# RWKV-7 attention and a hard-swish FFN on one core: three slots a unit on three PSUM pairs, with half turns

## The chip, the cores and the metric

The kernel runs on one NeuronCore of a Trainium2 chip. The metric is the device time of one launch in microseconds (us). Engines are named as in the profile: PE is TensorE's matmuls, PEld its weight loads, DVE VectorE, ACT ScalarE, POOL GpSimd, and SP the engine whose queue issues most DMAs.

## What is computed

All values are float32. The attention has B = 4, H = 8, T = 768 steps, D = 40, one 40 x 40 state for each batch row and head:

```python
for t in range(S):
    y[:, :, t] = np.einsum('bhd,bhde->bhe', rt, state)
    Sa = np.einsum('bhde,bhe->bhd', state, at)
    state_decay = state * wt[:, :, None, :] - np.einsum('bhd,bhe->bhde', Sa, bt)
    state = state_decay + np.einsum('bhd,bhe->bhde', vt, kt)
```

Its output, reordered to 3072 tokens x 320 features, goes through an FFN of width 2048:

```python
h = x @ w_in                       # 320 -> 2048
g = h * np.clip(h + 3.0, 0.0, 6.0) / 6.0
return g @ w_out                   # 2048 -> 320
```

## The kernel before

**Units.** The sequence is cut into chunks of 64 steps. A unit is 64 steps of two batch rows, with the two rows in the two halves of the 128 partitions: 24 units, 0 to 23, four to a group. Units i and i + 2 share a state. Each unit passes through two sets of stages. `prepare` doesn't need the state and runs ahead: W (turn the decays, scan them), gam (the second scan; factors gam and rgam), A, B and K (turn the input, multiply by a factor), F and E (products of these), factor (turn rgam, scale K and B on POOL), EV. `step` needs the state: RT, VT and S (turns of r, v and the state), R, U, UT, C, rS, H, then sn (the state's update) and y; move and move2 send y to the FFN's input xt by DMA. Once a group, `invert` inverts a triangular 32 x 32 system for all its heads on DVE, a chain of 60 small products and sums (L741, L747) between transposes (fb at the start, tb and tt at the end); `third_block` completes the inverse on PE (L776, L799).

**Turns.** A turn is a transpose on PE. `turn_pairs` (L474) does four 128 x 128 transposes into one bank; `turn_halves` (L484) does eight with 64 rows each, the two batch rows going to the two banks of a pair. From unit 8 on A, B, R, V and rgam (L643) are turned by halves, and W, K and the state (L878) are turned whole.

**FFN jobs.** A unit gives two jobs, (i, 0) and (i, 1), half of the hidden columns each. `expand` writes the hidden values to two banks "h" (L1054: 16 full 128-row products and 8 on half the rows, the "narrow" ones, issued by `short`). ACT (L1069) and DVE (L1070) make gt of them. `contract` (L1095) multiplies gt by w_out into the bank "o", 8 products of 320 columns. A float32 product leaves two records in the trace. The contract of a job is issued after the expand of the next job. The sum of a unit stays in "o" over both jobs, and ACT (L1113) copies it to ob once per unit, from where a DMA takes it out; units 0 and 1 are split into two sums.

**PSUM and order.** There are eight banks: "one" (1), "pair" (two pairs, 4), "o" (1), "h" (2). The order is written out by the program, with no scheduler behind it. From unit 4 on a unit has four blocks. In a block, `together` issues the PE products of all stages that are due, first for the state stages, then for those that run ahead, closing a batch (`finish`, which issues the copies out of PSUM on ACT and DVE) when five banks are in use. Between them `feed` issues pieces of the FFN: a piece is one step of the generator `feed_forward`, four FFN tiles of `expand` or two or so products of `contract`. While an inversion is open (`side`), `aside` issues two of its steps with each piece. Each engine executes its own list strictly in the order of issue.

Of the kernel before, what the change touches and what calls it, by code (L numbers as in the profile page):

```python
# [31 lines left out]
def kernel(  # L32
# [64 lines left out]
    def bank(tag, shape, bufs):  # L97
        return ps.tile(shape, F32, name=tag, tag=tag, bufs=bufs)

    ring, open_half = deque(), [None]  # L100
    lent = tc.tile_pool(name="lent", bufs=1, space=PSUM)
    pools = {"lent": lent.__enter__(), "pair": ps}
    pairs = deque([("pair", 2), ("pair", 2), ("lent", 1)])
# [7 lines left out]
    def begun_ffn():  # L111
# [4 lines left out]
        pools["h"] = ctx.enter_context(tc.tile_pool(name="hidden", bufs=1, space=PSUM))  # L116


    def ps_any(shape):
# [404 lines left out]
    def prepare(i, F):  # L524
        n, o = i % NU, data[i]
        halves = i >= 2 * NU
        def w_stage():
            wt = turn_pairs(o["WN"])
            yield PE

            wm = o["wm"] = wms[i % 2]
            wv = wm[:, 0:SCAN].rearrange("p (r m i) -> p r m i", m=2, i=HB + 1)
            x = wt[:].rearrange("p r (q m i) -> p (r q) m i", q=2, m=2)
            if i == 0:
                nc.vector.tensor_copy(wv[:, :, 0, 1:HB + 1], x[:, :, 0, ::-1])
            else:
                nc.scalar.activation(out=wv[:, :, 0, 1:HB + 1], in_=x[:, :, 0, ::-1], func=AF.Copy)
            if i == 0:
                nc.vector.tensor_copy(wv[:, :, 1, 1:HB + 1], x[:, :, 1, :])
            else:  # L540
                nc.scalar.activation(out=wv[:, :, 1, 1:HB + 1], in_=x[:, :, 1, :], func=AF.Copy)  # L541
            fetch("W", following(i))
            prods = o["prods"] = tmp.tile([P, NB, 2, HB + 1], F32, name="prods", bufs=2)
            nc.vector.tensor_tensor_scan(  # L544
                out=prods[:].rearrange("p r m i -> p (r m i)"), data0=wm[:, 0:SCAN], data1=start[:],
                initial=0.0, op0=ALU.mult, op1=ALU.add,
            )
# [89 lines left out]
        def factor_stage():  # L637
# [23 lines left out]
            for x, name in enumerate("KB"):  # L661
# [4 lines left out]
                )  # L666
            if i > 2 * NU:
                fetch("V", i)
# [3 lines left out]
        def k_stage():  # L672
            x = turn_pairs(o["KN"])
            yield PE
            kt = o["kt"] = turned("kt")
            nc.vector.tensor_tensor(out=kt[:], in0=x[:], in1=o["rg"][:], op=ALU.mult)

        def e_stage():
            x = scores(o["kt"], o["at"])
            yield PE  # L680
            o["E"] = masked(x)

        def ev_stage():
# [82 lines left out]
    def third_block(F, tb, tt, n, zs, first=False):  # L766


        parts = [slice(0, H)]
        zp = ps_pair(H, L)  # L770
        for h in range(H):
# [20 lines left out]
        shared[0] = None  # L792
        yield DONE
        tp = ps_pair(H, L)
        for h in range(H):
# [24 lines left out]
    def step(i):  # L820
# [52 lines left out]
        def s_S():  # L873

            sp = ps_any([P, 2, 2, P])
            for q in range(2):
# [171 lines left out]
    def expand(xt, j0, gts):  # L1048
# [9 lines left out]
        def short():  # L1058
            narrow.clear()
            for i in range(NQ):  # L1060
                for c in range(2):
                    add(c, i, win2[half(c), (j0 + i) * P:(j0 + i + 1) * P], xt[half(c), 2, :])
            if begun[0] + begun[1] == 6 * NQ:
                results()

        def results():
            for c in range(2):
                gt = ffn.tile([P, NQ, P], F32, name="gt", bufs=5)
# [6 lines left out]
        for c in range(2):  # L1075
            for t in range(2):
                for i in range(NQ):
                    j = c * HJ + j0 + i
                    add(c, i, win[:, t, j * P:(j + 1) * P], xt[:, t, :])
                if c == 1 and t == 1 and not narrow:  # L1080
                    results()
                yield True
        if not spread[0] and narrow:
# [3 lines left out]
    def contract(i, r, gts):  # L1087
        split = i < SPLIT
        if r == 0 or split:
            op = bank("o", [P, 512], 1)[:, 0:DM]  # L1090
        else:
            op = sums.pop(i)
        for c in range(2):
            for n in range(NQ):
                nc.tensor.matmul(out=op[:], lhsT=gts[c][:, n, :],  # L1095
                                 rhs=wout[:, c * HJ + r * NQ + n, :],
                                 start=((split or r == 0) and c == 0 and n == 0),
                                 stop=((split or r == 1) and c == 1 and n == NQ - 1))
                if n % 2 and (c == 0 or n < NQ - 1):
                    yield True  # L1100
        if r == 0:
            sums[i] = op
            if split:
                part = ffn.tile([P, 3 * P], F32, name="part", tag="xt", bufs=6)[:, 0:DM]
                nc.scalar.activation(out=part, in_=op[:], func=AF.Copy, scale=1.0 / 6.0)
                sums[i] = part
        else:
            ob = ffn.tile([P, DM], F32, name="ob", bufs=OB)
            if split:
                nc.vector.scalar_tensor_tensor(out=ob[:], in0=op[:], scalar=1.0 / 6.0,  # L1110
                                               in1=sums.pop(i), op0=ALU.mult, op1=ALU.add)
            else:
                nc.scalar.activation(out=ob[:], in_=op[:], func=AF.Copy, scale=1.0 / 6.0)  # L1113
            del ready[i]
            g, p = names[i]
            for q in range(2):
                row = (2 * p + q) * T + g * BL
                queue = nc.scalar if q and i == NK - 1 else nc.sync
                queue.dma_start(out=out[row:row + BL, :], in_=ob[half(q)])
        yield True  # L1120


    RGT, OB = 2, 1
    stream = feed_forward()
    weights = load_weights()
# [3 lines left out]
    def pieces(n):  # L1129

        owed[0] += n * (8 / 9 if spread[0] else 1)
        while owed[0] >= 1:
            owed[0] -= 1
            if not next(stream):
                owed[0] = 0.0
# [192 lines left out]
    def together(stages):  # L1328
# [3 lines left out]
        def finish():  # L1332
# [4 lines left out]
            begun.clear()  # L1337
            shared[0] = open_half[0] = None
            ring.clear()
            ring.extend(TURNS_IN)  # L1340

# [52 lines left out]

    m = 0
    for i in range(NU, NK):
        spread[0] = i >= 2 * NU - 1
        for j in range(BLOCKS):
            rate, inversion = 3.5, 0
            if i + AHEAD >= NK + NU - 1:  # L1400
                rate = 4.5
            if i < 2 * NU - 1:
                rate = 2.8
            parts = a_block(m)
            next(parts)
            if side or i % NU == NU - 1 and rate < 4:

                rate, inversion = 6.2, 2 + (i < 2 * NU)
            feed(rate / 2, inversion)
            for _ in parts:  # L1410
                pass
            if i % NU < 2 and j < 2:
                if i % NU == 0:
                    aside(3 * L)
                block(i, j)
            if side:
                rate, inversion = 6.2, 2 + (i < 2 * NU)
            feed(rate / 2, inversion)
            m += 1
    for _ in range(2):  # L1420
        for _ in a_block(m):
            pass
        m += 1
    spread[0] = False
# [32 lines left out]
```

## Time and profile before

| | us |
|---|---|
| median of 3 runs | 797.86 |
| lowest and highest | 796.54 to 798.12 |
| span of the profiled execution, first to last instruction | 802.0 |

The profile gives the profiled execution no time beside its span; the span is 4.1 us, 0.5%, over the median. Other rows that the steps use, of whole groups: L1054 busy 250.4 us, L1095 231.8 us, L1070 62.0 us (mean 681 ns), L555 37.6 us (1565 ns), L544 30.3 us (1270 ns), L520 49.9 us (723 ns), L1113 9.6 us (435 ns). Matmuls are pipelined: the mean of one L1054 record is 282 ns, but the next begins after some 112 ns, so costs on PE are read from starts, not from durations.

### The profile page before, as it was taken

How to read it: one execution, taken by the hardware profiler on the slowest of the kernel's cores; microseconds unless marked ns; L12 is line 12 of the kernel's file. 1: busy time of each engine (PE TensorE's matmuls, PEld its weight loads, DVE VectorE, ACT ScalarE, POOL GpSimd, SP SyncE). 2: the span in 40 equal slices, each digit the busy share in tenths (PEclk: the TensorE clock that was granted, in tenths of full speed). 3: DMA queues.
4: the chain of work that ended last, by engine and by line, in shares of the span. 5: the costliest groups of instructions: out<-in, count | busy, mean ns of one | idle time of the engine just before them, and what ended most of it. 6: DMA issues, size and time to landing. Idle time of an engine off the chain costs nothing.

```text
span 802.0 us, 35325 instructions
## 1 busy us (share of the span) xinstructions
PE 733.3 (91%) x15832; PEld 622.8 (78%) x15832; DVE 495.5 (62%) x967; ACT 321.2 (40%) x668; POOL 175.6 (22%) x318
## 2 busy tenths in 40 slices
PE   5726777999999989999999999999999999999998
PEld 4625665878778868888888888888888888888886
DVE  7896777679555699455698445897444973322210
ACT  2348882321644424543344453324443324422111
POOL 6403012420322222223123123304122202000000
PEclk9855798999999999999999999999999999999999
DMA  9683553420233331233222233213222101110000
GB/s 120 118 198 85 152 142 57 76 46 9 45 57 66 59 56 28 53 64 56 41 45 43 44 58 62 46 34 57 44 51 48 20 20 29 30 25 13 15 19 17
DMA packets 174215, 45.03 MB, mean 56 GB/s; under 512 B 157424, under 2 KB 172784, under 8 KB 174064
## 3 DMA queue, kind: packets, MB, share of 16 engines
q1 hardware_dynamic: 169760, 42.03, 27.7%
q8 instruction: 125, 2.05, 1.1%
q10 hardware_dynamic: 4304, 0.74, 0.7%
q14 instruction: 26, 0.21, 0.1%
HBM read 34.08 MB, written 3.93 MB: 47 GB/s over the span
## 4 chain that ended last, share of the span: by engine, by line
PE 77%; DVE 8%; issue 5%; DMA 4%; SPq 2%; ACT 2%; POOL 1%; DVEq 0%; ACTq 0%; POOLq 0%
PE h L1054 26%; PE o L1095 24%; PE pair L512 4%; PE pair L972 3%; PE pair L484 2%; PE pair L949 2%; PE one L474 2%; PE pair L894 2%; PE pair L856 2%; PE pair L914 1%; PE pair L690 1%; PE pair L930 1%; DMA R<-in_r_dram 1%; DVE wm L555 1%; PE pair L799 1%
## 5 line engine op out<-in xcount | busy, mean ns | idle before, releaser
L1054 PE MATMUL h<-xt,win 128*128 128x128 f32 (+1 forms) x2304 | 250.4, 282 | 3.5 <-DVE gt L1070 3.5
L1054 PEld LDWEIGHTS h<-xt,win 128*128 128x128 f32 (+1 forms) x2304 | 230.8, 192 | 20.5 <-issue 4.2
L1095 PE MATMUL o<-wout,gt 128*128 128x320 f32 x768 | 231.8, 445 | 0.0
L1095 PEld LDWEIGHTS o<-wout,gt 128*128 128x128 f32 x768 | 139.2, 191 | 51.0 <-issue 1.2
L1070 DVE SCALAR_TENSOR_TENSOR gt<-gt,h 128x512 f32<-128x512 f32 x96 | 62.0, 681 | 71.7 <-ACT gt L1069 71.6
L1069 ACT ACTIVATE gt<-h,three 128x512 f32<-128x512 f32 x96 | 62.2, 686 | 100.9 <-PE h L1054 100.5
L984 POOL TENSOR_TENSOR yg<-ys,gam 128x512 f32<-128x512 f32 x22 | 39.0, 1772 | 165.4 <-DVE ys L983 91.2
L741 DVE TENSOR_TENSOR prod<-x 128x30 f32<-128x30 f32 (+9 forms) x180 | 67.2, 373 | 8.8 <-POOL x L726 3.3
L663 POOL TENSOR_TENSOR KBt<-K,rgt 128x320 f32<-128x320 f32 x22 | 19.0, 865 | 215.4 <-ACT rgt L652 166.9
L747 DVE TENSOR_TENSOR x<-x,prod 128x30 f32<-128x30 f32 (+9 forms) x180 | 62.3, 346 | 5.5
L957 DVE TENSOR_TENSOR state<-pair,state 40x320 f32<-40x320 f32 (+1 forms) x44 | 21.4, 487 | 65.9 <-PE pair L949 39.8
L520 DVE COPY_PREDICATED score<-mask,pair 128x512 f32<-128x512 int32 x71 | 49.9, 723 | 1.8 <-PE pair L512 1.4
L983 DVE TENSOR_TENSOR ys<-pair,ys 128x512 f32<-128x512 f32 x22 | 15.2, 691 | 44.7 <-PE pair L690 22.0
L555 DVE TENSOR_TENSOR_SCAN wm<-wm,start 128x528 f32<-128x528 f32 x24 | 37.6, 1565 | 0.8
L544 DVE TENSOR_TENSOR_SCAN prods<-wm,start 128x528 f32<-128x528 f32 x24 | 30.3, 1270 | 10.2 <-ACT wm L541 10.1
L834 ACT ACTIVATE RT<-pair 128x512 f32<-128x512 f32 x21 | 12.5, 597 | 52.9 <-PE pair L484 52.9
L972 PE MATMUL pair<-score,KBt 64*64 64x64 f32 x1472 | 29.2, 232 | 4.0 <-DVE state L957 3.2
L695 ACT ACTIVATE EV<-pair 64x320 f32<-64x320 f32 x44 | 19.0, 432 | 33.5 <-PE pair L690 22.8
L972 PEld LDWEIGHTS pair<-score,KBt 64*64 64x64 f32 x1472 | 25.8, 145 | 6.6 <-DVE state L957 3.7
L809 ACT ACTIVATE tinv<-pair 32x256 f32<-32x256 f32 x48 | 18.0, 375 | 30.1 <-PE pair L799 29.5
L1113 ACT ACTIVATE ob<-o 128x320 f32<-128x320 f32 x22 | 9.6, 435 | 49.1 <-PE o L1095 29.3
L572 POOL COPY gam<-prods 128x256 f32<-128x256 f32 x24 | 22.5, 937 | 29.3 <-DVE prods L544 25.4
(262 smaller groups left out, 1062.6 us busy)
## 6 DMA issues: line engine op xcount, KB each, us to landing
V<-in_v_dram SPq DMA_DIRECT2D x96, 40.0 KB
out_dram<-ob SPq DMA_DIRECT2D x47, 80.0 KB
R<-in_r_dram SPq DMA_DIRECT2D x92, 40.0 KB
B<-in_b_dram SPq DMA_DIRECT2D x42, 80.0 KB
K<-in_k_dram SPq DMA_DIRECT2D x42, 80.0 KB
W<-in_w_dram SPq DMA_DIRECT2D x37, 80.0 KB
A<-in_a_dram SPq DMA_DIRECT2D x37, 80.0 KB
xt<-yg SPq DMA_DIRECT2D x72, 40.0 KB
```

The lines of the kernel that those rows point to most:

```text
L512: nc.tensor.matmul(out=o[i][half(q), n, :], lhsT=lhs[half(i, D), n ^ (2 * q * swap), half(q)], rhs=rhs[half(i, D), n, half(q)], start=True ...
L520: nc.vector.copy_predicated(out=x[:].rearrange("p (i h) t -> p i h t", i=2), mask=mask8, data=o[2])
L544: nc.vector.tensor_tensor_scan(out=prods[:].rearrange("p r m i -> p (r m i)"), data0=wm[:, 0:SCAN], data1=start[:], initial=0.0, op0=ALU.m ...
L555: nc.vector.tensor_tensor_scan(out=back, data0=back, data1=start[:], initial=0.0, op0=ALU.mult, op1=ALU.add)
L741: nc.vector.tensor_tensor(out=pv, in0=_ap(x[:], (i + 1) * L + i, [[L, n], [0, i]]), in1=_ap(x[:], i * L, [[0, n], [1, i]]), op=ALU.mult,)
L747: nc.vector.tensor_tensor(out=rest, in0=rest, in1=pv, op=ALU.add)
L972: nc.tensor.matmul(out=y[q][half(s), pr, :], lhsT=o[name][half(q), h * D:h * D + SLOT], rhs=m[name][half(q), 4 * rs + 2 * s + j, :], start ...
L984: nc.gpsimd.tensor_tensor(out=yg[:], in0=m["ys"][:].rearrange("p r q t -> p r (q t)"), in1=o["G"][:], op=ALU.mult)
L1054: nc.tensor.matmul(out=hp[c][:, i, :], lhsT=lhsT, rhs=rhs, start=(begun[c] == 0), stop=(begun[c] == 3 * NQ - 1))
L1069: nc.scalar.activation(out=gt[:], in_=hp[c][:], func=AF.Relu, bias=three[:], scale=1.0)
L1070: nc.vector.scalar_tensor_tensor(out=gt[:], in0=gt[:], scalar=6.0, in1=hp[c][:], op0=ALU.min, op1=ALU.mult)
L1095: nc.tensor.matmul(out=op[:], lhsT=gts[c][:, n, :], rhs=wout[:, c * HJ + r * NQ + n, :], start=((split or r == 0) and c == 0 and n == 0), ...
```

## The change

From unit 8 on:

- W and K (from unit 13 on, `late`) and the state (from unit 8 on) are turned by halves, like the other inputs.
- "one" and "o" are given up and become a third pair, "extra". A unit has three slots, and a slot is a batch of fixed stages that fills exactly three pairs, in the order pair, extra, pair.
- A slot stands at one of two places of an FFN job: after the third piece of an expand ("e3"), or after a contract ("end"). Between two slots go the pieces from one place to the next; while an inversion is open, from e3 to e3, a whole job of eight pieces, with 2.25 steps of the inversion for each piece.
- `contract` writes to the first bank of "extra". Each job's sum leaves PSUM by itself: for r == 0 ACT copies it to ob, for r == 1 DVE adds the second sum to it there. This holds for every unit from 2 on, before unit 8 with the bank "o".
- gt of the first half of the hidden columns is made as soon as its products are issued (`results(c)`), not with the second half.
- The V of a late unit is fetched behind its E stage, no longer behind factor.

The core of the diff:

```diff
+    THREE = [("pair", 2), ("extra", 1), ("pair", 2)]
+    def begun_slots():
+        single.__exit__(None, None, None)
+        del pools["single"]
+        pools["extra"] = ctx.enter_context(tc.tile_pool(name="extra", bufs=1, space=PSUM, side="right"))
+        ring.clear()
...
-            wt = turn_pairs(o["WN"])
+            wt = turn_halves(o["WN"])[2] if late else turn_pairs(o["WN"])
...
-            x = turn_pairs(o["KN"])
+            x = turn_in(o["KN"], late)
...
+            if i >= 2 * NU:
+                sp = ps_pair(4, BL)
+                for n in range(4):
+                    for x in range(2):
+                        nc.tensor.transpose(
+                            out=sp[x][:, n, :], identity=ident[half(x), half(x)],
+                            in_=st[half(x), n // 2, 2 * (n % 2):2 * (n % 2) + 2, :].rearrange("p r d -> p (r d)"))
...
-        if r == 0 or split:
+        if "extra" in pools:
+            op = pools["extra"].tile([P, 2, 512], F32, name="extra", tag="extra", bufs=1)[:, 0, 0:DM]
+        else:
             op = bank("o", [P, 512], 1)[:, 0:DM]
-        else:
-            op = sums.pop(i)
...
+            part = sums.pop(i)
+            ob = ffn.tile([P, DM], F32, name="ob", bufs=OB)[:] if split else part
+            nc.vector.scalar_tensor_tensor(out=ob, in0=op[:], scalar=1.0 / 6.0, in1=part, op0=ALU.mult, op1=ALU.add)
...
+    SLOTS = [
+        [(0, "RT VT"), (4, "K factor"), (-1, "H"), (4, "F")],
+        [(0, "S"), (5, "W"), (0, "R"), (-1, "sn"), (3, "EV"), (4, "E"), (-1, "y"), (-1, "move move2"), (5, "gam")],
+        [(5, "A B"), (0, "rS C U UT")],
+    ]
+    AFTER = [
+        "factor K VT RT H F y".split(),
+        "R sn EV y E S W move move2 gam".split(),
+        "A B rS C U UT".split(),
+    ]
+    STEPS_OF = 2.25
+    def piece():
+        place[0] = next(stream)
+        if side:
+            steps_due[0] += STEPS_OF
+            aside(int(steps_due[0]))
+            steps_due[0] -= int(steps_due[0])
+        return place[0] is not None
+    def gap(dense, between={}):
+        n = 0
+        stop = "end" if place[0] == "e3" and not dense else "e3"
+        while piece():
+            n += 1
+            if n in between:
+                between[n]()
+            if place[0] == stop:
+                break
...
+    for i in range(2 * NU, NK + 3):
+        for j in range(3):
+            slot(i, j)
...
+            gap(bool(side), between)
```

In `SLOTS` the number is the unit's distance from i; `AFTER` is the order in which the copies out of PSUM are issued on ACT and DVE. `slot` first issues the narrow products of the open expand, then all PE products of the slot, then these copies.

## The prediction

> **What bounds the kernel now.** I read the page's totals and slices first.
>
> ```profile
> PE 733.3 (91%) x15832; PEld 622.8 (78%) x15832; DVE 495.5 (62%) x967; ACT 321.2 (40%) x668; POOL 175.6 (22%) x318
> PE   5726777999999989999999999999999999999998
> DVE  7896777679555699455698445897444973322210
> PEclk9855798999999999999999999999999999999999
> ```
>
> From a third of the span on, which is where the change begins (unit 8 starts near 318 us), TensorE is full at full clock. DVE peaks where an inversion runs. The windows by 50 us say the same:
>
> ```profile
> 400.00:450.00 50.00, 49.80 (x1122) 42.41 (x1119) 41.12 (x82) 22.23 (x47) 13.01 (x18) 1.00 0.25 48
> 500.00:550.00 50.00, 49.29 (x871) 42.22 (x869) 43.07 (x93) 16.55 (x36) 10.46 (x19) 1.00 0.22 40
> ```
>
> So only what shortens TensorE's list, or makes it wait, counts. The timeline of PE prices the list; starts subtract (a f32 matmul leaves two records, a transpose one):
>
> ```profile
> 397.71 0.60 PE L474 MATMUL one<-ident,W 128*128 128x128 f32 x4
> 398.24 1.16 PE L1054 MATMUL h<-xt,win 64*128 64x128 f32 x16
> 399.23 0.41 PE L484 MATMUL pair<-ident,R 64*128 64x64 f32 x8
> 399.47 0.42 PE L484 MATMUL pair<-ident,V 64*128 64x64 f32 x8
> 399.82 1.16 PE L972 MATMUL pair<-score,KBt 64*64 64x64 f32 x64
> ```
>
> A whole turn takes 0.53 us, a half turn 0.24 us before another half turn and 0.35 before products. Last, TensorE against DVE in an inversion:
>
> ```profile
> 507.55 0.69 PE L512 MATMUL pair<-RT,UT 40*64 40x64 f32 x32
> 508.64 2.42 PE L1095 MATMUL o<-wout,gt 128*128 128x320 f32 x8
> ```
>
> ```profile
> 508.82 0.98 DVE L957 TENSOR_TENSOR state<-pair,state 40x320 f32<-40x320 f32 x2
> 509.84 1.35 DVE L520 COPY_PREDICATED score<-mask,pair 128x512 f32<-128x512 int32 x2
> 511.08 0.37 DVE L747 TENSOR_TENSOR x<-x,prod 128x130 f32<-128x130 f32 x1
> ```
>
> DVE has emptied what L512 made (E's products end at 508.7, not shown) only at 511.2, 2.5 us later, with gt and the state adds in front, and TensorE doesn't notice: the FFN product L1095 has the bank "o" to itself.
>
> **Gain: the list.** The order of instructions shows 38 turns changed (W 11, K 11, S 16). They stand beside other half turns, so each falls from 0.53 to between 0.24 and 0.30; I take 0.26, 38 x 0.27 = 10.3 us. Leaving products for the FFN costs 0.12 (L512 VT: 0.605 before L1054, 0.487 before another product); such exits from unit 8 on fall from 65 to 50: 1.8 us. Entering half rows from FFN matmuls costs 0.10 (a run of eight L1054 records takes 0.995 before the half rows or L1095, 0.891 before a whole turn), and whole turns had been entered free: 26 entries more, 2.6 us. Net 9.5 us less. Everything else on TensorE keeps its number of matmuls, and 14 FFN jobs stand before unit 8's S in both.
>
> **Nearly free.** The FFN sum of r == 0 leaves by ACT (0.43 us, L1113), that of r == 1 by a DVE scalar_tensor_tensor over 320 columns, a form that the trace shows only at the start; between 0.40 (the spacing of L860, 320 columns) and 0.59 (of L1070, 512) I take 0.45. Twenty-two of them add 10 us to DVE, which has room except in inversions. The out DMA now must have read "ob" one job (over 9 us) after it was sent, not two; sending takes 1.2 us (L1119), so it is hidden unless SP is blocked. V is fetched behind E instead of factor, a unit ahead of EV: hidden. The xt moves now follow y in the same slot, so SP waits about 2.2 us for POOL's L984 with little behind it; for jobs 22, 30 and 38, the first of unit 11, 15 and 19, sending (3.1 us) and landing end about when the job begins. I take 0, with 3 us each as the far end.
>
> **Cost: the third pair.** "extra" holds the second pair of a slot, then op of the contract that follows an e3 slot, then (after an end slot) the next slot's second pair. So TensorE, four FFN tiles after a slot (0.99 us), waits for whoever empties "extra". Queued behind that wait is everything that TensorE does. A result is read only when all stages of its tile are done (L834's R waits for V, L898's U for UT).
>
> Slot 2 (A B, rS C, U UT): short 1.00, then 0.24 + 0.35 + 0.47 + 0.49 + 0.49 + 0.61, e4 0.99: the contract wants "extra" 4.6 us after the slot starts. On DVE stand gt 0.6, A 0.6, B 0.6 and the mask of C 0.65 before it is free, 2.5 us. It waits when DVE comes more than 2.0 us late.
>
> In units 11 and 15 DVE does. All spacings are from the timelines of DVE and ACT. Slot 0: DVE clears K at 3.1, then stands until 4.8 for POOL's scale, which is queued behind two KBt products (0.87 each), then state and H to 6.0; ACT has F's six copies (0.36 each) done at 5.95 and the second relu (0.6) behind them, so gt ends at 7.2. The transpose fb and its way through POOL take 2.8 (502.11 to 504.87), then 15 inversion steps 5.5, so DVE is free 15.5 us after the slot began. TensorE needs 3.2 (slot with short) + 0.99 + 4.4 (contract) + 2.8 (three quarters of the next expand) = 11.4. Lag 4.1. Slot 1: gt 0.6, R 0.4, two state adds 0.9: "extra" free at 6.15 against 5.83 wanted, wait 0.3. Then y 0.6, E 0.65, and W with gam 4.1 (two scans and two copies, 402.11 to 406.21), gt 0.6, 18 steps of 0.42 (2.25 a piece, eight pieces) and the sum 0.45: DVE ends at 20.0, TensorE reaches slot 2 at 13.3. Lag 6.6, less the 2.0: wait 4.6. Per inversion 4.9, twice 9.8; unit 19 has no W left and pays about 1.0. Together 10.8.
>
> Smaller ones, by the same kind of sum. In units 10, 14 and 18 slot 2 starts at "end" and the sum of r == 1 stands on DVE behind gam and gt: these end at 11.0 from slot 1's start, the sum at 11.5, and 0.14 later (gt to L1054, 406.89 to 407.03) the bank is free; TensorE wants it at 10.9 to 11.0: 3 x 0.65 = 2.0. At unit 8 the first "extra" tile waits for a sum behind tb and tt (to 318.8 in the trace; y wanted at 318.2): 1.2. In units 12, 16 and 20 ACT's four tinv copies (0.375 each) stand ahead of the sum: 3 x 0.5 = 1.5. In the last units H (three times 0.6), or sn with y (0.7), sits in "extra" right before a contract: 2.5; elsewhere the turn of op to the slot after "end" takes 0.73 (L1095's end 406.82, ACT done 407.35, 0.14 more) against 0.60 to 0.68 until it is wanted: a dozen such, 1.0. That is 8.2 at most. Each is below 1.3 us and rests on ends that are modelled, so I count half, 4.1.
>
> Sum: -9.5 + 10.8 + 4.1 = +5.4 us. The profiled span was 802.0, 0.5% over the median 797.86; there it would be 807.4. I carry the difference to the median: 803.3.
>
> A rule against the change: the Trainium skill, "Perfetto Trace Analysis", Optimizing Tensor Performance, has independent matmul groups rotate through PSUM banks so that evacuation overlaps the next group. By that rule every slot would pay for its evacuation; by the rows only one where DVE is over 2.0 us late does, and the sum above goes by the rows.
>
> **Rivals.** 1. Faster: the evacuations of "extra" come in time, the list alone decides, 788.4. It holds if DVE's lag at slot 2 stays under 2.0 us. For it: outside inversions DVE is busy under half of the time (24.39 of 50 us from 450), and TensorE waits on DVE hardly at all now. Against: 2.5 us of lag are visible already with two steps a piece. With half the lag the result is about 795.
> 2. Slower still, by the clock. A wait of 3.2 us cost more than itself:
>
> ```profile
> 129.20:132.00 2.80, 0.00 (x0) 0.00 (x0) 2.74 (x7) 0.00 (x0) 0.01 (x1) 0.86 0.40 65
> 132.00:138.00 6.00, 5.61 (x71) 4.32 (x72) 1.70 (x4) 0.00 (x0) 0.00 (x0) 0.50 0.36 71
> 134.30 4.25 PE L1095 MATMUL o<-wout,gt 128*128 128x320 f32 x8
> ```
>
> Eight L1095 records took 4.25 instead of 2.25, and y, ahead of them, 1.9 instead of 1.1: 2.8 us. A gap of 3.75 us at 119 us left the clock at 1.00. If both long waits trip it, 2 x 2.8 = 5.6: 808.9. The Trainium skill, "TensorE: Matmul & The Clock Gate", Part 1, says that one idle window of about 3.4 us halves the clock; by that rule both waits would. Of the two gaps, one bears it out.
> 3. Break even: half the waits of slot 2 and none of the small ones, 9.5 against about 8: 797.
>
> **How the numbers follow.** Forecast (slower, clock kept) 0.43; rival 2 0.19; rival 1 with its half case 0.28; rival 3 0.10. A difference within 0.2%, 1.6 us, is about what a measurement here can't tell from none; so faster 0.28, same 0.10, slower 0.62. The forecast's own range is 799.5 to 807. For 8 in 10 I reach down to 792, which takes in half of rival 1, and up to 811, which takes in rival 2 and most of the small costs in full.
>
> **What would show it.** Right: the 38 turns at 0.24 to 0.30; PE idle of 4 to 5 us before a contract in units 11 and 15, released by DVE's mask of C; PE busy in those windows below 46 of 50. The gain step is wrong if half turns cost over 0.4, the cost step if no PE wait there exceeds 1 us. The forecast fails if DVE clears its steps earlier than its queue suggests, or if xt lands late at jobs 22, 30 and 38.

## The result, and the profile after

The changed kernel takes 844.58 us (median of 4 runs, 838.51 to 845.90), the one before, run beside it, 797.62 us (796.54 to 798.12). The ratio is 1.0576, interval 1.0538 to 1.0613: 47 us slower, where the prediction had 5.4. The sign was right, the size far off.

The page of the changed kernel, its totals, its slices and the head of the chain that ended last:

```profile
PE 737.8 (87%) x15984; PEld 623.9 (74%) x15984; DVE 501.3 (59%) x989; ACT 327.0 (39%) x668; POOL 167.4 (20%) x318
PE   5627759999999899899798889898998899999997
DVE  7896786698555994545965435876345774322221
PEclk9955789999999999999999999898999999999999
PE 44%; issue 18%; DVE 17%; ACT 7%; SPq 5%; DMA 4%; POOL 4%; POOLq 0%; ACTq 0%; DVEq 0%
```

TensorE's row now has eight 8s and a 7 between slices 16 and 31 (338 to 675 us), its clock has dips, and TensorE itself carries 44% of the chain, where it carried 77%. "issue", time in which an engine waits for nothing that the profile shows, is 18%, where it was 5%. The two windows that were full before (length; busy time of PE, PEld, DVE, ACT and POOL, with the number of records; granted clock, DMA share, GB/s):

```profile
400.00:450.00 50.00, 40.76 (x773) 34.73 (x773) 38.48 (x85) 15.41 (x30) 8.89 (x13) 0.97 0.21 39
500.00:550.00 50.00, 45.49 (x1008) 38.81 (x1007) 34.05 (x70) 15.90 (x35) 10.80 (x21) 0.93 0.27 51
```

What TensorE waits for from unit 8 on, from the table of waits (sum in us, times, longest; shortened to its head):

```profile
PE pair L1020 <- issue: 8.0, 6, 1.8
PE extra L1143 <- ACT EV L729: 6.6, 3, 2.7
PE pair L811 <- ACT wm L556: 4.9, 2, 2.5
PE extra L1143 <- DVE score L537: 4.8, 5, 3.1
PE pair L811 <- issue: 3.7, 4, 1.1
```

In the changed kernel L1143 is `contract`, L1020 y, L811 the first product of `third_block`, L1102 `expand`, L537 the masks, L501 a half turn. The second and fourth line are the predicted kind: the contract waits until "extra" is emptied. The third, a wait for W's pair, was not foreseen (e2 below), and the first and the fifth are of a kind that wasn't in the prediction at all.

To add up, I take the stretch from the first product of the contract of the fifteenth FFN job (early in unit 8) to TensorE's last product. Both kernels have the same 34 jobs there. "Gaps" are TensorE's idle times of over 0.1 us, by what ended them; "list" is the rest; "half clock" is time at a granted clock of 0.5. All columns but the median are of the one profiled execution, which lay up to 3.3 us from the median of its kernel (that of before 4.4 us by its span, nearly all of it ahead of the stretch: e4, the same kernel up to unit 8, comes to it 3.5 us earlier).

| kernel | median us | stretch | list | gaps: issue | gaps: ACT, DVE | half clock |
|---|---|---|---|---|---|---|
| before | 797.6 | 437.7 | 435.6 | 1.5 | 0.7 | 0 |
| after | 844.6 | 481.6 | 444.5 | 16.4 | 20.8 | 23.9 |
| e1_split | 846.3 | 482.1 | 447.5 | 4.5 | 30.1 | 20.5 |
| e2_copies_first | 836.3 | 473.8 | 441.6 | 16.1 | 16.1 | 17.1 |
| e7_copies_steps | 841.7 | 479.2 | 443.3 | 15.5 | 20.4 | 20.5 |
| e6_copies_e2 | 825.4 | 461.5 | 437.0 | 14.6 | 9.8 | 10.2 |
| e14_e2_split | 825.7 | 460.7 | 438.8 | 8.6 | 13.2 | 3.4 |
| e11_e2_pool_sum | 829.6 | 465.4 | 441.7 | 13.8 | 9.8 | 20.5 |
| e3_no_chain | 812.3 | 453.8 | 432.2 | 16.3 | 5.3 | 0 |
| e5_split_no_chain | 811.4 | 453.1 | 439.3 | 3.9 | 9.8 | 3.4 |
| e10_half_products | 797.3 | 440.6 | 423.1 | 8.4 | 9.1 | 6.8 |
| e12_room | 809.2 | 450.0 | 432.7 | 15.7 | 1.6 | 3.4 |
| e13_room_split | 807.5 | 447.2 | 436.4 | 7.0 | 3.8 | 0 |
| e8_before_sums | 800.6 | 438.3 | 436.3 | 0.9 | 1.2 | 0 |
| e4_before_merged | 798.6 | 437.9 | 436.0 | 1.2 | 0.7 | 0 |
| e9_before_halves | 839.3 | 475.0 | 450.6 | 0 | 24.4 | 30.7 |

After against before, the stretch is 43.9 us longer: 14.9 of waits that end in "issue", 20.1 of waits for ACT and DVE, and 8.9 of list, of which about 12 are matmuls at half clock (half of 23.9), so that the list itself became some 3 us shorter (e3, which has the same list and no half clock: 432.2 against 435.6). The other 3 us lie before the stretch, where the changed kernel has a wait of 1.2 us for the sum at unit 8, as the prediction had it, a stop of 1.8 us (shown next) and a dip of the clock at 349 us.

**The wait nobody predicted.** TensorE at the end of slot 1 of unit 9 (start, length, engine, line, what it writes and reads; in brackets the idle time before it and what ended that), and one queue's packets, MB and share in a window of 1.3 us inside it:

```profile
344.33 0.70 PE L529 MATMUL pair<-at,kt 40*64 40x64 f32 x32
344.82 0.56 PE L1020 MATMUL pair<-score,KBt 64*64 64x64 f32 x21
347.19 0.91 PE L1020 MATMUL pair<-score,KBt 64*64 64x64 f32 x43 [1.81 <-issue]
348.03 0.71 PE L1102 MATMUL h<-xt,win 128*128 128x128 f32 x4
```

```profile
q8 instruction: 1, 0.02, 4.6%
```

y stops after 21 of its 64 records, in the middle of one stage, with all of its operands there; in this window the queue q8, "instruction", moves one packet of 16 KB, from 344.76 to 345.72. q8 has 126 packets in the whole run and TensorE 32248 records (matmuls, weight loads and 280 semaphore and drain instructions, which have to be counted too): one packet for 256 records. I counted the records up to every idle time of this kind of over 0.3 us, 18 of them in the late stage: all 18 end at record 193 or 194 of a block of 256, and each ends 1.3 to 1.6 us after a packet of q8 has landed. A block that ends in such a stall was run in 2.5 to 4.2 us with the stall. Slot 1 asks for 480 records (its densest 480 took 3.7 us); the densest 480 of the kernel before took 6.1 us. The packets didn't get slower: in the late stage the middle one took 1.0 us, in the kernel before 1.05. The reading that fits all of this is that TensorE ran out of instructions. The trace of before has three such stops (0.87, 0.51 and 0.98 us, at 338.8, 543.6 and 580.8), all at 193 of 256 too.

### The profile page after: what moved, and what is told of

Its sections match the earlier page's. It is cut to its first block, busy times and chain, and to the rows that moved or that the text cites. A ratio compares the mean times of both kernels' runs of the same rounds, so it can differ in the third digit from the quotient of the medians.

```text
span 844.1 us, 35603 instructions
## 1 busy us (share of the span) xinstructions
PE 737.8 (87%) x15984; PEld 623.9 (74%) x15984; DVE 501.3 (59%) x989; ACT 327.0 (39%) x668; POOL 167.4 (20%) x318
## 4 chain that ended last, share of the span: by engine, by line
PE 44%; issue 18%; DVE 17%; ACT 7%; SPq 5%; DMA 4%; POOL 4%; POOLq 0%; ACTq 0%; DVEq 0%
PE h L1102 15%; PE extra L1143 10%; PE o L1143 4%; DVE prod L775 3%; DVE x L781 3%; SPq L475 2%; POOL KBt L694 2%; DVE score L537 2%; PE pair L529 2%; SPq L472 2%; DMA raw<-in_moe_w_out_dram 2%; DVE prods L575 2%; DVE gt L1118 2%; PE pair L1020 1%; ACT F L664 1%
## 5 line engine op out<-in xcount | busy, mean ns | idle before, releaser
L1102 PE MATMUL h<-xt,win 128*128 128x128 f32 (+1 forms) x2304 | 253.1, 284 | 5.1 <-DVE gt L1118 2.7
L1102 PEld LDWEIGHTS h<-xt,win 128*128 128x128 f32 (+1 forms) x2304 | 231.8, 193 | 19.2 <-issue 3.2
L1143 PE MATMUL extra<-wout,gt 128*128 128x320 f32 x576 | 174.9, 458 | 12.9 <-ACT EV L729 6.6
L1143 PEld LDWEIGHTS extra<-wout,gt 128*128 128x128 f32 x576 | 112.3, 201 | 62.4 <-issue 8.6
L1032 POOL TENSOR_TENSOR yg<-ys,gam 128x512 f32<-128x512 f32 x22 | 29.6, 1347 | 197.5 <-DVE ys L1031 96.6
L1143 PE MATMUL o<-wout,gt 128*128 128x320 f32 x192 | 58.9, 445 | 0.0
L537 DVE COPY_PREDICATED score<-mask,pair 128x512 f32<-128x512 int32 x56 | 40.2, 723 | 10.3 <-ACT ys L984 10.0
L1143 PEld LDWEIGHTS o<-wout,gt 128*128 128x128 f32 x192 | 34.1, 189 | 12.3
L1020 PE MATMUL pair<-score,KBt 64*64 64x64 f32 x1216 | 24.7, 222 | 9.4 <-issue 8.0
L1020 PEld LDWEIGHTS pair<-score,KBt 64*64 64x64 f32 x1216 | 21.7, 136 | 11.5 <-issue 8.7
L729 ACT ACTIVATE EV<-extra 64x320 f32<-64x320 f32 x24 | 10.4, 432 | 45.2 <-DVE state L1005 42.6
L797 POOL COPY tinv<-tb 32x1024 f32<-32x1024 f32 x10 | 10.3, 1034 | 74.0 <-DVE tb L784 73.7
L1154 ACT ACTIVATE ob<-extra 128x320 f32<-128x320 f32 x18 | 7.8, 435 | 43.8 <-PE extra L1143 43.7
L1159 DVE SCALAR_TENSOR_TENSOR ob<-extra,ob 128x320 f32<-128x320 f32 x18 | 8.8, 487 | 26.1 <-PE extra L1143 26.1
```

Of the source, the lines that this page charges most:

```text
L537: nc.vector.copy_predicated(out=x[:].rearrange("p (i h) t -> p i h t", i=2), mask=mask8, data=o[2])
L1020: nc.tensor.matmul(out=y[q][half(s), pr, :], lhsT=o[name][half(q), h * D:h * D + SLOT], rhs=m[name][half(q), 4 * rs + 2 * s + j, :], start ...
L1032: nc.gpsimd.tensor_tensor(out=yg[:], in0=m["ys"][:].rearrange("p r q t -> p r (q t)"), in1=o["G"][:], op=ALU.mult)
L1102: nc.tensor.matmul(out=hp[c][:, i, :], lhsT=lhsT, rhs=rhs, start=(begun[c] == 0), stop=(begun[c] == 3 * NQ - 1))
L1143: nc.tensor.matmul(out=op[:], lhsT=gts[c][:, n, :], rhs=wout[:, c * HJ + r * NQ + n, :], start=(c == 0 and n == 0), stop=(c == 1 and n == ...
```

## The experiments

Expectations that were written ahead count idle times from unit 8's start (18.2 us of "issue", 22.6 of ACT and DVE); the table starts a little later.

**e1_split.** Slot 1 cut in two:

```diff
+            if j == 1 and names_ == "EV":
+                for name in "R sn EV S".split():
+                    ... (their copies out of PSUM)
+                place[0] = next(stream)
```

> The changed kernel with slot 1 cut in two: behind the evacuation of the units' C the copies of R, sn and S are made and one FFN piece is put in, and only then come E and y; the products of the third block move one FFN piece back. Nothing is left out. Theory A, instruction supply: the 16 to 19 idle stretches of PE in the late stage that end in "issue" (18.2 us in all) come because slot 1's some 480 PE records are run in 3.6 us, faster than blocks of 256 records arrive; with a piece of long matmuls in the middle they fall to 6 us or less, the dips of the granted clock behind them (at 349 and 451 us) go, and the time falls by 12 to 22 us, to 823 to 832. Theory B, those stretches are waits on data or PSUM that the trace does not name, in the order of the slot: they stay, and the time is within 3 us of the changed kernel's (842 to 848).

846.29 us (845.88 to 848.03). The idle times that end in "issue" went as theory A said, 16.4 to 4.5, so density of records is what makes them. The time didn't follow, and that is theory B's number. The same place of the trace:

```profile
345.92 1.16 PE L1102 MATMUL h<-xt,win 128*128 128x128 f32 x8
347.01 0.69 PE L529 MATMUL pair<-at,kt 40*64 40x64 f32 x32
347.52 0.40 PE L1020 MATMUL pair<-score,KBt 64*64 64x64 f32 x13
348.37 1.03 PE L1020 MATMUL pair<-score,KBt 64*64 64x64 f32 x51 [0.45 <-issue]
```

The stop of 1.81 us is down to 0.45, but waits on ACT and DVE grew by 9.3 us, probably because E, y and gam now come a piece later, and the list by 3.0, though there is 3.4 us less half clock in it.

**e2_copies_first.** ACT's copies of S and W ahead of EV:

```diff
+            if name == "sn":
+                for other, x in begun:
+                    if other == "S":
+                        ... (its copy)
+                    if other == "W":
+                        next(x)
```

> The changed kernel with ACT's copies of S and of W in slot 1 issued ahead of its copies EV of the state turn; nothing else is moved. Theory A, serialised evacuation: EV waits 42.6 us in 11 places for DVE's state sums in the same tile, and S's and W's copies stand behind EV in ACT's order, so W's scan and its pair of PSUM are late. Then PE's waits for W's pair at 448 and 579 us (2.5 and 2.4 us) and the dips of the granted clock behind them vanish: 6 to 10 us less, 834 to 839. Theory B, the loss is instruction supply alone: 0 to 2 us less, and the idle stretches that end in "issue" keep their 18 us. Both agree that those 18 us stay here.

836.30 us, inside theory A's range. This is what was in the way, ACT and TensorE in the changed kernel:

```profile
448.24 0.88 ACT L729 ACTIVATE EV<-extra 64x320 f32<-64x320 f32 x2 [2.11 <-DVE state L1005]
449.12 0.60 ACT L920 ACTIVATE S<-pair 128x512 f32<-128x512 f32 x1
449.62 0.80 ACT L556 ACTIVATE wm<-pair 128x256 f32<-128x256 f32 x2
```

```profile
450.47 0.75 PE L811 MATMUL pair<-tb,F 32*32 32x32 f32 x64 [2.51 <-ACT wm L556]
```

EV and sn share the second pair of slot 1, so ACT's EV stands until DVE has added sn to the state, and S and W, whose results lay ready, stand behind it. With the order changed the two waits for W's pair are gone, and 8 us with them.

**e3_no_chain.** The inversion's DVE steps left out, for the last three groups as it was meant:

```diff
         for i in range(1, L - 1):
+            if len(group_F) > 3:
+                yield
+                yield
+                continue
```

> The changed kernel without DVE's 60 small products and sums of the inversion in the last three groups of the stage (that part of the computation is left out), so that DVE has about 0.25 us times 60 = 15 us less to do in units 8 to 19 and nothing stands ahead of the masks of C. Theory A, late evacuation is the main loss: PE's waits on ACT and DVE fall from 22.6 to under 8 us, at most three dips of the granted clock are left, the time falls by 20 to 28 us, to 817 to 825. Theory B, instruction supply is the main loss: the waits that end in "issue" stay at about 18 us with the dips behind them, and the time falls by about 5 us.

812.34 us, 32 us less, more than theory A's 20 to 28. But the trace shows that the edit left out more than it says: 126 of 360 steps remain, so that 54 of the 60 that ran at 275 to 308 us, ahead of unit 8, went too. On the stretch, which holds only the last three inversions, it is 27.8 us less. There waits on ACT and DVE fall to 5.3 us and every dip of the clock goes; the "issue" waits stay, as both theories said. TensorE's waits now begin:

```profile
PE pair L1024 <- issue: 9.0, 6, 1.8
PE h L1106 <- issue: 2.9, 3, 1.1
PE pair L815 <- issue: 2.7, 4, 1.3
PE pair L529 <- issue: 2.1, 2, 1.5
```

So late evacuation, which came from DVE's inversion steps, and the half clock behind it make up nearly two thirds of the loss on the stretch, 27.8 of 43.9 us. 16.1 us are left. (e5, e10, e12 and e13 hold the same edit; their times, too, gain some us ahead of the stretch, and only the stretch compares with the kernel before.)

**e4_before_merged.** In the kernel before, the FFN pieces between the two parts of a block moved behind the second part.

```diff
-            feed(rate / 2, inversion)
             for _ in parts:
                 pass
+            feed(rate / 2, inversion)
```

> The kernel before, with one edit from unit 8 on: the FFN pieces that lay between the two parts of a block are put behind the second part, so that two parts of short matmuls (some 400 PE records) follow one another; no turn, pair or evacuation is changed. Theory A, instruction supply: PE's idle stretches that end in "issue" grow from 2.4 us to 10 us or more in the late stage, each starting again at the first records of a block of 256 (193 of 256, as in both traces), and the time rises by more than these 8 us where the clock dips too: 806 to 825. Theory B, no limit of supply: PE's new waits name ACT and DVE only, and those that end in "issue" stay below 4 us.

798.55 us, ratio 0.9999 (0.9985 to 1.0012), and no new stops. The kernel didn't do what it was made for: its densest 400 records took 4.01 us, those of before 4.02 us; in the changed kernel it is 2.65 us. It says only that merging parts up to that density costs nothing, and doesn't test either theory.

**e5_split_no_chain.** e1's and e3's edits together.

```diff
+            if j == 1 and names_ == "EV": ... place[0] = next(stream)
+            if len(group_F) > 3: yield; yield; continue
```

> The changed kernel without the 60 DVE steps of the inversion in the last three groups (that part of the computation is left out) and with slot 1 cut in two by an FFN piece. Against the kernel that only leaves out the DVE steps (812.3 us). Theory A, instruction supply costs time wherever late evacuation does not: its 18.5 us of PE idle that end in "issue" fall to about 6 and the time falls by 9 to 13 us, to 799 to 803, near the kernel before. Theory B, the cut costs as much as it saves in every case, because E and y and their evacuation come a piece later: within 3 us of 812, with the ACT and DVE waits up by as much as the issue waits are down.

811.39 us, where 799 to 803 was expected by theory A: theory B by the time. "issue" fell from 16.3 to 3.9 us, but ACT and DVE waits rose by 4.5 and the list by 7.1. That isn't theory B's account either, which had the waits rise by all that the stops fell: the larger part went into the list, 5.4 us for the cut and 1.7 for one dip of the clock.

**e6_copies_e2.** e2, and the slot stands after the second piece of an expand:

```diff
-        stop = "end" if place[0] == "e3" and not dense else "e3"
+        stop = "end" if place[0] == "e2" and not dense else "e2"
```

> The changed kernel with the S and W copies ahead of EV (836.3 us so) and with the place e3 of an FFN job moved one piece forward: the slot stands after the second piece of an expand, so that eight FFN tiles (about 2.2 us) and not four lie between a slot and the contract that wants the pair extra. Nothing is left out. Theory A, the contract's waits are late evacuations of extra: each of the waits of 1.7 to 2.7 us before a contract shrinks by about 1.2 us, ACT and DVE waits fall from 16.9 to 9 or less, the dips of the granted clock behind them get fewer, and the time falls by 6 to 14 us, to 822 to 830; the issue waits stay at 18. Theory B, the same lag shows up at the next user, the slot after end, which is now only two pieces away: ACT and DVE waits and the time stay within 3 us.

825.41 us (822.34 to 833.71), theory A: 11 us less than e2 for one more piece between a slot and the contract that wants "extra". The waits before the contract are gone but for one of 0.9 us; those of 1.8 to 2.3 us that are left stand before the slot that follows a contract, for the sum (L1160) that DVE makes late, such as

```profile
409.83 0.96 PE L979 MATMUL extra<-RT,S 40*64 40x64 f32 x32 [1.80 <-DVE ob L1160]
```

**e7_copies_steps.** e2, with 2.5, 1.0 and 3.0 inversion steps a piece after the slots 0, 1 and 2 in place of 2.25.

```diff
-    STEPS_OF = 2.25
+    STEPS_OF = [2.5, 1.0, 3.0]
-            steps_due[0] += STEPS_OF
+            steps_due[0] += STEPS_OF[after_slot[0]]
```

> The changed kernel with the S and W copies ahead of EV (836.3 us so), and with the inversion's DVE steps dealt otherwise over the pieces: 2.5 a piece after slot 0, 1.0 after slot 1, 3.0 after slot 2, in place of 2.25 everywhere; their number is the same. Nothing is left out. Theory A, the wait of the contract behind slot 2 comes from DVE's queue of W, gam and 18 steps between slots 1 and 2 (predicted 4.6 us, 1.7 measured with the copies first): those two waits (417 and 547 us) vanish, and the time falls by 3 to 8 us unless the slots after the denser gaps wait in turn, which would show as DVE waits before the contract behind slot 0 or slot 1. Theory B, DVE's sum of work over the whole inversion is what is late: the waits only move, the time stays within 3 us.

841.65 us, 5 slower than e2. The two waits behind slot 2 vanished; three of 2.4 us came up before the contract behind slot 0 (at 427, 557 and 685 us), and those behind slot 1 grew from 2.0, 2.7 and 2.3 to 2.6, 3.5 and 2.8. That is the exception that theory A named, and theory B's reading: dealing the steps otherwise moves the waits.

**e8_before_sums.** The kernel before, with each job's FFN sum leaving "o" by itself.

```diff
-        if r == 0 or split:
-            op = bank("o", [P, 512], 1)[:, 0:DM]
-        else:
-            op = sums.pop(i)
+        op = bank("o", [P, 512], 1)[:, 0:DM]
...
+            nc.vector.scalar_tensor_tensor(out=ob, in0=op[:], scalar=1.0 / 6.0, in1=part, op0=ALU.mult, op1=ALU.add)
```

> The kernel before with one part of the change alone, from unit 2 on: each job's FFN sum leaves the bank o by itself, by ACT for r == 0 and by a DVE addition for r == 1; turns, pairs and the order of everything else are those of before. The prediction's term for this part was 0 (about 10 us more on DVE, hidden): within 1.6 us of 797.6. Rival, the additions stand in DVE's way during the inversions or the next contract waits for its bank: 3 to 10 us slower, with PE waits on ACT or DVE at the contract.

800.56 us; ratio 1.0022 (1.0003 to 1.0042), 1.7 us against the kernel before in the same session. The predicted 0, with its 1.6 us of margin, is missed by a hair; the rival's 3 to 10 isn't reached, though the interval just touches it (0.2 to 3.4 us).

**e9_before_halves.** The kernel before, with the half turns alone (W and K of late units, the state from unit 8 on), in the two pairs; the narrow products of an open expand go ahead of these turns.

```diff
-            wt = turn_pairs(o["WN"])
+            wt = turn_halves(o["WN"])[2] if late else turn_pairs(o["WN"])
-            x = turn_pairs(o["KN"])
+            x = turn_in(o["KN"], late)
...
+            if i >= 2 * NU:
+                sp = ps_pair(4, BL)
```

> The kernel before with another part of the change alone: W and K from unit 13 on and the state from unit 8 on are turned by halves, into halves of the two pairs, and the narrow products of an open expand go ahead of the first half turn; blocks, two pairs, the bank o and its sums stay. Theory A, the list gain is real and survives without the third pair: the 33 turns of the late stage cost 7.0 us less (17.0 to 10.0 us between starts, as measured in the changed kernel), of which 2 to 4 go to further changes between FFN and half rows: 3 to 6 us less than before, 792 to 796. Rival, the turns now share the two pairs with the products, so that batches wait for evacuation of a pair: ACT and DVE waits of PE above 5 us in all, and no faster than before.

839.26 us: the rival, and far beyond it. The turns got cheaper as counted (17.0 to 10.1 us), though the list, with half clock counted at half, is only 0.3 us shorter. But TensorE waits

```profile
PE pair L512 <- DVE at L603: 19.7, 11, 2.7
PE pair L638 <- DVE kt L692: 5.7, 11, 1.1
```

because C and F now take the pair that A, B and K hold until DVE has emptied it. Of the nine waits for A on the stretch two, of 2.7 us, end behind inversion steps; the other seven, of 1.2 to 2.0 us, come where no inversion runs. The whole turns in "one" were dear on the list, but kept these stages out of each other's way.

**e10_half_products.** e3, and from unit 8 on without the products with B in sn and y.

```diff
-            for name in "KB":
+            for name in ("K" if i >= 2 * NU else "KB"):
```

> The changed kernel without the 60 DVE steps of the inversion in the last three groups (812.3 us so), and from unit 8 on also without the products with B in sn and y: slot 1 then has 352 in place of 480 PE records. These parts of the computation are left out. The products left out take about 0.42 and 0.55 us each between starts, for some 15 units 14.5 us together. Theory A, instruction supply: with slot 1 that much shorter in records, the 18.5 us of idle that end in "issue" fall to 8 or less as well, and the time falls by 22 to 28 us, to 784 to 790. Theory B, these idle stretches cost nothing of themselves or have another cause: the time falls by the products alone, 13 to 16 us, to 796 to 799.

797.32 us (793.69 to 800.87), 15.0 less than e3: theory B by the time. "issue" halved (16.3 to 8.4), ACT and DVE waits rose by 3.8; the list fell by 9.1, though the products left out were 12.5, with 6.8 us of half clock against it.

**e11_e2_pool_sum.** e6, with the sum of r == 1 by an ACT copy and a POOL addition (`rgt` has one buffer in place of two).

```diff
+                nc.scalar.activation(out=more[:], in_=op[:], func=AF.Copy, scale=1.0 / 6.0)
+                nc.gpsimd.tensor_tensor(out=ob, in0=more[:], in1=part, op=ALU.add)
```

> The changed kernel with the S and W copies first and slots one piece earlier (825.4 us so), and from unit 8 on the FFN sum of r == 1 leaves extra by an ACT copy, with the addition on POOL, in place of the DVE addition (the buffer for it is won by one rgt buffer in place of two). Nothing is left out. Theory A, what is left of the waits (8.4 us, after contracts: PE waits for the extra that DVE's addition has to empty behind its queue) goes away with the dips behind it: 8 to 13 us less, 812 to 817, and then the issue waits of 17 us are what separates the kernel from the one before. Theory B, DVE is late for the masks and state sums too, so the waits show at the next one: within 3 us of 825.

829.55 us (826.96 to 831.94): no gain. The waits for the sum went, waits of 3.0 and 3.3 us before a contract came back, and the clock was at half for 20.5 us. Theory B's place was right, its 3 us nearly (4.1); the one rgt buffer is a second difference, so how much of it is DVE's lag stays open.

**e12_room and e13_room_split.** e3, e2 and e6 together (no steps, copies first, slots a piece earlier): uncut, and with slot 1 cut.

> The changed kernel with room for the evacuations on three sides: without the 60 DVE steps of the inversion in the last three groups (left out), with the S and W copies ahead of EV, and with the slots one piece earlier. Slot 1 is whole. Theory A, the supply costs by itself: ACT and DVE waits fall from 6.0 us (in the kernel without the steps, 812.3 us) to 3 or less, the issue waits stay at 16 to 19, and the time is 807 to 811. Theory B, the supply's waits only stand in front of late evacuations: with room the issue waits get no smaller, but the time falls to 800 or less.

> The kernel with room for the evacuations (no inversion steps on DVE in the last three groups, which is left out; S and W copies first; slots one piece earlier) and with slot 1 cut by an FFN piece. Theory A, the supply costs by itself: the issue waits fall by 11 to 13 us, ACT and DVE waits stay below 4, the cut adds 3.5 us for 16 times two further changes between FFN and half rows (0.10 and 0.12 us each), and the time is 7 to 10 us below that of the same kernel uncut. Theory B: the time stays within 3 us of the uncut kernel's.

e12: 809.23 us, theory A's numbers (15.7 us of stops on the stretch, where 16 to 19 were expected from unit 8 on). It is the cleanest kernel of the series: TensorE waits 1.6 us for ACT and DVE, its list is 2.9 us shorter than before's, and still the stretch is 12.3 us longer. The rest is 14.2 us more of

```profile
PE pair L1025 <- issue: 9.4, 6, 2.2
PE pair L529 <- issue: 2.7, 2, 1.7
PE pair L816 <- issue: 2.3, 3, 1.0
```

e13: 807.47 us; the ratios to before, 1.0115 (1.0091 to 1.0139) and 1.0104 (1.0072 to 1.0136), can't be told apart, which is theory B's time and not theory A's 7 to 10 us less. "issue" fell by 8.7, not the 11 to 13 expected, the list rose by 3.7 (expected 3.5) and ACT and DVE waits by 2.2: 2.8 us less on the stretch. With half clock counted at half, the cut adds 4.5 to 5.4 us to the list in all four pairs (e1, e5, e13 and e14 against after, e3, e12 and e6). So a cut by an FFN piece costs nearly as much as it saves. That the stops cost what they last rests on the sum for e12; no run took them away and left all else alone.

**e14_e2_split.** The same as e13 with nothing left out.

> The changed kernel, nothing left out, with the S and W copies first, the slots one piece earlier and slot 1 cut by an FFN piece: the best of the edits together. Uncut it took 825.4 us. If the supply costs by itself (theory A): 815 to 821, with issue waits of 5 us in place of 16.7. If the inversion's steps on DVE are what is left (theory B): within 3 us of 825.4, with DVE waits above 12 us. Neither expects it below the kernel before.

825.65 us, equal to e6's 825.41: 6.0 us less "issue", 3.4 more ACT and DVE waits. Theory B. The best versions of the changed kernel are 26 us behind the kernel before; no experiment pointed to one that beats it.

## Why the prediction was wrong

**Half turns: right by the piece.** The timeline of TensorE in unit 9:

```profile
363.10 0.46 PE L501 MATMUL pair<-ident,R 64*128 64x64 f32 x8
363.40 0.41 PE L501 MATMUL pair<-ident,V 64*128 64x64 f32 x8
363.70 0.46 PE L501 MATMUL extra<-ident,K 64*128 64x64 f32 x8
364.00 0.41 PE L674 MATMUL extra<-ident,rgam 64*128 64x64 f32 x8
```

They start 0.30 us apart, in the range given. On the stretch the turns of W, K and the state took 10.0 in place of 17.0 us, 0.21 for each of some 33, not 0.27. The price of entering and leaving half rows was the weak part: predicted net 0.8 (2.6 less 1.8), here 3.6 as what remains of 7.0 when e3's list is 3.4 shorter; it wasn't read row by row. List gain 3.4 on the stretch, which holds 33 of the 38 turns, not 9.5.

**The third pair: right in kind, and in size partly by luck.** The wait predicted for unit 11, slot 2, TensorE and then DVE:

```profile
416.29 1.16 PE L1102 MATMUL h<-xt,win 128*128 128x128 f32 x8
420.54 6.20 PE L1143 MATMUL extra<-wout,gt 128*128 128x320 f32 x16 [3.10 <-DVE score L537]
```

```profile
417.21 0.41 DVE L781 TENSOR_TENSOR x<-x,prod 128x240 f32<-128x240 f32 x1
...
417.97 0.68 DVE L1118 SCALAR_TENSOR_TENSOR gt<-gt,h 128x512 f32<-128x512 f32 x1
418.60 0.67 DVE L619 TENSOR_TENSOR at<-pair,gam 128x512 f32<-128x512 f32 x1
...
419.78 0.71 DVE L537 COPY_PREDICATED score<-mask,extra 128x512 f32<-128x512 int32 x1
```

DVE finishes its inversion steps, then gt, A, B, and only then the mask of C, in the order that the prediction laid out; 4.6 us were predicted, 3.1 came here and 0.8 in unit 15. In turn slot 1's waits, predicted 0.3, were 1.8 and 2.7, and unit 19's 2.1 in place of 1.0. In unit 11 the two make 4.9, the sum predicted for an inversion, split otherwise between the slots; with unit 15 and unit 19 they make 10.5 us, where 10.8 were predicted. The prediction followed DVE's queue, but not ACT's: EV behind the state sums, with S and W behind EV (e2), wasn't seen, and the 4.9 us of waits for W's pair weren't in it. The rest, 5.4 us, are small ones, for which half of 8.2 had been counted. In all 20.1 us more of waits than before against 14.9 predicted.

By the rule quoted there from the Trainium skill, "Perfetto Trace Analysis", Optimizing Tensor Performance, independent groups should rotate through PSUM banks. The runs bear it out more than the prediction allowed: e9, which lets turns and products share two pairs, loses 24.4 us in waits, and e6's one more piece between a slot and its reuse of "extra" wins 11 us.

**The clock: in the wrong place.** Rival 2 priced it at two dips of 2.8 us, with a chance of 0.19. It came with five dips on the stretch, 23.9 us, worth about 12. TensorE in the 3.4 us after the wait of 3.1, and further on (columns as in the windows above; the products differ, the granted clock, 0.52 and 1.00, is what compares):

```profile
420.54:424.00 3.46, 3.46 (x7) 2.29 (x8) 3.22 (x9) 0.00 (x0) 0.00 (x0) 0.52 0.00 0
426.60:430.00 3.40, 3.40 (x35) 3.28 (x35) 1.37 (x5) 0.44 (x1) 0.00 (x0) 1.00 0.00 0
```

A wait of 1.8 us can be enough (the last section has the count), so nearly every large wait of the sum should have carried the price of a dip. The gap of 3.75 us at 119 us, which the prediction set against rival 2, was one of the rare ones that cost none: by the phase of that run's dips it fell on a border between two clock windows, with 1.95 us in one and 1.80 in the next.

**The step that failed** is the cost term: it held waits for evacuation alone. "Everything else on TensorE keeps its number of matmuls" was true and beside the point, because the same matmuls were packed closer than their instructions arrived, and a block of 256 records with a stop took 2.5 to 4.2 us. That term was put at nothing, and measured 14.9 us. The clock was left out of the sum as well (about 12 us), and the list gain was sized at 9.5 where it was 3.4. With what was measured the sum reads -3.4 + 20.1 + 14.9 + 12 = 43.6 us, against 43.9 measured on the stretch; the prediction had -9.5 + 14.9 + 0 + 0. The range left out the clock beyond two dips and the supply altogether.

**The rest.** FFN sums per job at 0: 1.7 us (e8). V's later fetch and the xt moves: no wait of TensorE in the late stage names a DMA or SP, as predicted. Break even and rival 1 needed evacuations in time; e3 and e12 show that even then the stretch is 16.1 and 12.3 us longer.

The table also shows where e5 and e10 lost what they saved in "issue". In e5 12.4 us of stops went, against 4.5 us more of ACT and DVE waits, 5.4 for the cut and 1.7 of half clock; in e10 7.9 went, against 3.8 and 3.4 of half clock. What stays open is why the waits for ACT and DVE rise each time that the stops fall. That the stops of TensorE had been giving those engines time to catch up fits this, but no run separates it from the later start of E and y.

## What to carry to other kernels

When an edit packs small matmuls closer together, count records per microsecond as well as matmuls: look in the trace of before for stops that end in "issue" at equal distances in the record count; three short ones were there to see. Before PSUM is shared more tightly, follow the queue of every engine that empties it, ACT's as well as DVE's, to the moment when the next user wants the bank, at its busiest stage. Idle time of TensorE that adds up to over half of one clock window (1.7 of 3.4 us here) mostly costs itself and a dip.

## What the runs showed of the hardware

Instruction supply: one q8 packet of 16 KB stands for 256 TensorE records (126 packets for 32248; a float32 matmul is two matmul and two weight load records). Where the next block isn't there, TensorE stands until 1.2 to 1.6 us after the packet has landed, 2.2 to 3.0 us after its transfer began, and always at place 193 or 194 of 256: so in all 118 stops of this kind of over 0.3 us from 300 us on in nine kernels (before, after, e1, e2, e3, e6, e10, e12, e13).

The clock is decided on a fixed grid. Within a run every dip from 300 us on begins at the same phase of 3.413 us and lasts one or two such windows, but for one at the run's end. Over nine kernels (after, e1, e2, e6, e7, e9, e11, e12, e14) 35 of the 38 windows with TensorE idle for 1.7 us or more were followed by one at half clock, and 6 of the 72 with 1.0 to 1.7 us; with less, none was but the second windows of five dips. A wait of 1.81 us at 345.4 fell into one window and cost a dip; one of the same length at 403.0 fell on a border (0.4 and 1.4 us) and cost none. The Trainium skill, "TensorE: Matmul & The Clock Gate", Part 1, tells of a free-running window of 4096 cycles, about 3.4 us, which agrees, and of one idle window that halves the clock; here half a window idle was enough.
